# Merging a gMLP out projection into the following attention and projecting Q/K in token chunks: a four-layer kernel on one Trainium2 core

## The chip, the core and the metric

The kernel runs on one core of a Trainium2 chip. The metric is device time in microseconds (us), median of several runs, lower is better. The kernel before takes 1348.54 us (1347.62 to 1350.77, four runs).

TensorE does matmuls, VectorE, ScalarE and GpSimd do elementwise work, and SyncE only issues DMAs. Each of these engines works through its own queue of instructions. A DMA is issued by one of the queues of SyncE, GpSimd or ScalarE. The profile marks a queue as SPq (SyncE), POOLq (GpSimd) or ACTq (ScalarE).

## The reference, cut to what matters

Four layers alternate, A B A B, over x of shape 2048 x 576. A is attention with 32 heads of width 18, where each row attends to 8 rows, two apart. B is a gated MLP with a spatial matmul.

```python
def A(x):                                    # x = x + A(layernorm(x))
    q, k, v = split(x @ wqkv)                # 576 -> 3 * 576
    # row s attends to rows s, s-2, ..., s-14; softmax; times v
    return o @ wo

def B(x):                                    # x = x + B(layernorm(x))
    z = gelu(x @ w_in)                       # 576 -> 4608
    z1, z2 = z[..., :2304], layernorm(z[..., 2304:])
    g = w_sp @ z2 + b_sp                     # [2048, 2048] @ [2048, 2304]
    return (z1 * g) @ w_out                  # 2304 -> 576
```

## The kernel before

Activations are kept normalised and transposed in `xnT` (features on partitions). Five stages follow each other:

1. Attention 1. Rows are handled in 19 tiles of 112, each with a halo of 16 earlier rows, and each tile in two halves of 16 heads: 38 steps.
2. z2 projection (16 tiles of 128 rows) and spatial matmul (18 feature blocks) of the first B.
3. Out projection of the first B, then attention 2.
4. z2 projection and spatial matmul of the second B.
5. Out projection of the second B, and the output.

Q and K come out of the projection with seven heads stacked in one staging tile. The logits need each head at its own partition offset, so a small DMA per head copies it there. Q/K are made in two blocks of 1024 rows: 64 such copies per attention, dealt to three queues.

```python
# PG: project 512 columns of Q or K; when a block of 1024 is complete, copy each head
for j7 in range(nh):                             # 7 heads (4 in the last group)
    dst_ap = QK[32 * rg:32 * rg + DH, :, g, PADL + cb_c0:PADL + cb_c0 + cb_w]
    src_ap = stg[r0 + DH * j7:r0 + DH * (j7 + 1), :, 0:cb_w]
    # in the steps: SyncE, GpSimd and ScalarE in turn; before them: SyncE and GpSimd
    ...

for s in range(NSTEP):                           # 38 steps
    EXP(s); MASK(s)                              # ScalarE, VectorE
    L_mm(s + 1)                                  # logits of the next step, high priority
    PV(s - 1); NORM(s - 1)                       # values, division
    for fn in table.get(s, []): fn()             # projections, row tails, filler matmuls
```

The tail of a tile (in `table`) is a chain through several engines. SyncE transposes the attention output by DMA, TensorE multiplies by `wo`, and VectorE adds the residual and takes the statistics. GpSimd then normalises, and SyncE transposes into `xnT`.

```python
nc.sync.dma_start_transpose(out=oT_t[:, :, :nq], in_=o_t[:nq, :])          # TAIL_A
...                                                                        # TAIL_B: wo, add, stats
nc.sync.dma_start_transpose(out=self.xnT[:, :, ...], in_=xn[:nrows, :])    # TAIL_C
```

Late steps also hold two filler ("junk") matmuls each, whose results are not used. The z2 norm is nine instructions per tile of rows (six on VectorE, three on GpSimd). W_out is loaded in 18 pieces: all of it after the first spatial stage, and the second half of it after the second.

The softmax here doesn't subtract the row's maximum and nothing guards it: scores larger than these inputs give would overflow.

## Time and profile before

The first view sums each engine's busy time in the five stages. Its columns are the window (us) and its length, then busy us with the count of instructions for TensorE, its weight loads, VectorE, ScalarE and GpSimd, and last the mean granted TensorE clock, the busy share of the DMA engines and GB/s.

```profile
...
core 0: us, PE busy (x) PEld busy (x) DVE busy (x) ACT busy (x) POOL busy (x), PEclk, DMA share, GB/s
0.00:188.00 188.00, 143.74 (x1840) 85.66 (x1841) 121.92 (x314) 96.77 (x130) 101.97 (x147) 0.96 0.68 141
188.00:605.00 417.00, 407.00 (x1912) 186.45 (x1911) 167.69 (x355) 92.68 (x165) 73.63 (x93) 1.00 0.16 35
605.00:849.00 244.00, 218.37 (x2421) 143.49 (x2420) 143.55 (x347) 101.93 (x135) 94.34 (x135) 0.95 0.65 151
849.00:1264.00 415.00, 407.32 (x1909) 186.84 (x1908) 167.57 (x354) 92.79 (x165) 73.13 (x93) 1.00 0.16 35
1264.00:1348.00 84.00, 73.47 (x580) 57.01 (x577) 15.75 (x34) 0.00 (x0) 13.36 (x21) 0.95 0.33 101
...
```

TensorE is busy in 407 of 417 us of a z2 and spatial stage. The room lies in the two attention stages (144 of 188 us and 218 of 244 us) and in the last stage.

Next come the waits of TensorE, one line for each thing waited for: total us, number of times, longest. First attention 1:

```profile
...
PE pw L582 <- DMA oT_142<-o_t_129: 4.0, 1, 4.0
PE pp L412 <- DMA xnT<-ln_xn_84: 3.3, 1, 3.3
...
```

the start of the z2 stage:

```profile
...
PE pz L812 <- DMA win2b<-in_B_w_in_dram: 3.6, 1, 3.6
...
```

and the out projection of the first and the second B:

```profile
...
PE po_6066 L941 <- DMA wout_b<-in_B_w_out_dram: 7.1, 6, 2.1
...
```

```profile
...
PE po_12694 L941 <- DMA wout_b<-in_B_w_out_dram: 3.0, 3, 1.0
```

So W_out arrives late twice and a part of the z2 weights once per stage. These are the waits that the change sets out to remove.

The last two views concern DMA issue. The first gives minimum/median/maximum duration in ns of one Q/K copy issue on SyncE, and the second a stretch of SyncE's queue in attention 1 (start, duration, queue, line, operation, count).

```profile
...
L76 SPq DMA_DIRECT2D QK<-stg x48: 786/787/1016, 38.3 to 773.5; - x48
...
```

```profile
...
104.49 1.23 SPq L568 DMA_TRANSPOSE oT_142<-o_t_131  x1
105.77 0.57 SPq L76 DMA_DIRECT2D xo<-in_A_x_dram  x1
106.44 2.51 SPq L76 DMA_DIRECT2D QK<-stg  x3
110.22 1.22 SPq L186 DMA_TRANSPOSE xnT<-ln_xn_84  x1
...
```

A copy holds the queue for 787 ns and a transpose for 1.2 us.

### The profile page before, as it was taken

Reading aid. Unit: us, or ns where it says so; the run is one execution under the profiler, and the core shown is the slowest. Engines: PE = TensorE matmul, PEld = TensorE weight load, DVE = VectorE, ACT = ScalarE, POOL = GpSimd, SP = SyncE. Lnnn points to the kernel's source line nnn. Section 1 sums busy time; section 2 is a strip of 40 time slices with the busy share of each in tenths; the row PEclk is TensorE's granted clock in tenths of the full one; section 3 lists DMA queues with packets and bytes.
Section 4 is the critical chain, followed back from the end, with each engine's and each line's share of the span. In section 5 each row is a group of like instructions: output and inputs, shape, how many; then the busy total and the mean of one; then the engine's idle time right before and its main releaser. Section 6 shows DMA issues by size and latency. Waiting matters only on the chain.

```text
span 1348.4 us, 21451 instructions
## 1 busy us (share of the span) xinstructions
PE 1249.9 (93%) x8656; PEld 659.5 (49%) x8656; DVE 616.5 (46%) x1402; ACT 384.2 (28%) x595; POOL 356.4 (26%) x487
## 2 busy tenths in 40 slices
PE   1999969989999999998998987899999999999997
PEld 0456644434444444445754655444444444444576
DVE  4468858843322332332534878588323223333221
ACT  2556726620011111001126665465101111100000
POOL 7445547830000000002141646488000000000111
PEclk9999989999999999997999999899999999999999
DMA  9449759020000000009653677861100000000232
GB/s 264 98 94 145 121 134 214 1 90 6 9 10 9 10 9 9 0 4 266 179 137 62 151 145 129 181 125 41 43 9 9 10 9 9 2 7 1 72 113 67
DMA packets 180128, 101.04 MB, mean 75 GB/s; under 512 B 138276, under 2 KB 162212, under 8 KB 180028
## 3 DMA queue, kind: packets, MB, share of 16 engines
q1 hardware_dynamic: 170208, 84.15, 28.1%
q10 hardware_dynamic: 6364, 8.55, 2.2%
q0 software_dynamic: 3456, 6.96, 2.2%
q8 instruction: 68, 1.11, 0.3%
q14 instruction: 32, 0.26, 0.1%
HBM read 41.16 MB, written 16.52 MB: 43 GB/s over the span
## 4 chain that ended last, share of the span: by engine, by line
PE 62%; DVE 11%; POOL 10%; issue 7%; DMA 6%; ACT 3%; SPq 1%; ACTq 0%; POOLq 0%; DVEq 0%
PE pg L904 36%; PE po L941 9%; DVE z_junkD L819 4%; PE pp L412 3%; DMA QK<-stg 2%; POOL ln_xn_84 L181 2%; POOL ln_xn_81 L181 1%; POOL ln_rstd L164 1%; POOL z_rstd L835 1%; POOL ln_xn_83 L181 1%; POOL ln_xn_82 L181 1%; DMA wout_b<-in_B_w_out_dram 1%; DMA wv_sb<-in_A_wqkv_dram 1%; DMA win2b<-in_B_w_in_dram 1%; DVE z_msq L828 1%
## 5 line engine op out<-in xcount | busy, mean ns | idle before, releaser
L908 DVE TENSOR_TENSOR g_tmp<-pg,bsp 128x512 f32<-128x512 f32 x144 | 99.4, 692 | 435.5 <-PE pg L904 423.9
L412 PE MATMUL pp<-xnT,wqk_sb 128*128 128x512 bf16 x400 | 100.7, 394 | 29.8 <-DMA xnT<-ln_xn_84 28.5
L812 PEld LDWEIGHTS <-xnT 128*128 128x128 bf16 x800 | 78.4, 98 | 97.0 <-issue 13.0
L812 PE MATMUL pz<-win2a,xnT 128*128 128x512 bf16 x384 | 103.1, 379 | 5.9 <-ACT zp L816 4.4
L164 POOL TENSOR_TENSOR ln_rstd<-ln_rstd,neg_half 112x1 f32<-112x1 f32 (+2 forms) x70 | 43.4, 621 | 152.3 <-DVE ln_rstd L163 152.1
L812 PE MATMUL pz<-win2b,xnT 128*128 128x512 bf16 x256 | 77.0, 386 | 6.9 <-DMA win2b<-in_B_w_in_dram 6.9
L816 ACT ACTIVATE zp<-pz 128x1024 bf16<-128x1024 f32 x64 | 65.0, 1020 | 44.6 <-POOL z2b_9746 L845 18.9
L412 PEld LDWEIGHTS <-wqk_sb 128*128 128x128 bf16 x400 | 36.9, 100 | 71.2 <-issue 36.0
L819 DVE CUSTOM_DVE_ANT_0 z_junkD<-zp 128x1536 bf16<-128x1536 bf16 x32 | 56.9, 1777 | 18.7 <-ACT zp L816 18.7
L370 PE MATMUL pv<-wv_sb,xnT 128*128 128x288 bf16 (+1 forms) x380 | 62.2, 286 | 0.2 <-DVE stg L418 0.2
L76 POOL DMA_DIRECT2D wout_b<-in_B_w_out_dram x14 | 7.5, 541 | 172.4 <-PE pg L904 172.4
L76 POOL DMA_DIRECT2D QK<-stg x52 | 31.5, 608 | 73.0 <-ACT stg L420 28.0
L584 DVE TENSOR_TENSOR x_new<-pw,xo 112x288 f32<-112x288 f32 (+1 forms) x76 | 33.5, 445 | 18.0 <-PE pw L582 10.7
L420 ACT CAST stg<-pp 128x512 bf16<-128x512 f32 x54 | 31.0, 585 | 37.4 <-PE pp L412 22.7
L370 PEld LDWEIGHTS <-xnT 128*128 128x128 bf16 (+1 forms) x380 | 33.5, 97 | 15.8 <-issue 1.4
L489 PE MATMUL L_ps<-QK 18*128 18x112 bf16 (+1 forms) x1216 | 32.0, 210 | 4.9 <-DMA QK<-stg 1.7
L418 DVE CAST stg<-pp 128x512 bf16<-128x512 f32 x26 | 18.0, 691 | 37.0 <-PE pp L412 33.5
L159 DVE BATCH_NORM_STATS2 ln_st<-x_new 112x6 f32<-112x288 f32 (+1 forms) x76 | 33.9, 449 | 1.2
L489 PEld LDWEIGHTS <-QK 18*128 18x128 bf16 (+1 forms) x1216 | 20.4, 93 | 25.6 <-issue 21.6
L845 POOL TENSOR_SCALAR z2b_3101<-zp,z_rstd,z_nmr 128x256 bf16<-128x256 bf16 x16 | 32.4, 2024 | 0.0
L845 POOL TENSOR_SCALAR z2b_9746<-zp,z_rstd,z_nmr 128x256 bf16<-128x256 bf16 x16 | 32.4, 2023 | 0.0
L904 PE MATMUL pg<-W_sb,z2b_3093 128*128 128x512 bf16 x128 | 28.4, 379 | 1.9 <-DVE z2b_3093 L848 1.9
(549 smaller groups left out, 2513.3 us busy)
## 6 DMA issues: line engine op xcount, KB each, us to landing
xres_73<-x_new SPq DMA_DIRECT2D x18, 252.0 KB
xo<-xres_74 SPq DMA_DIRECT2D x18, 252.0 KB
xres_75<-x_new SPq DMA_DIRECT2D x18, 252.0 KB
QK<-stg POOLq DMA_DIRECT2D x52, 72.0 KB, 3.8
win2a<-in_B_w_in_dram SPq DMA_DIRECT2D x2, 1728.0 KB
QK<-stg SPq DMA_DIRECT2D x48, 72.0 KB
wqk_sb<-in_A_wqkv_dram ACTq DMA_DIRECT2D x4, 576.0 KB
out_dram<-ob SPq DMA_DIRECT2D x16, 144.0 KB
```

The source lines that it names most:

```text
L164: nc.gpsimd.tensor_tensor(out=rstd[:nrows, :], in0=rstd[:nrows, :], in1=self.neg_half[:nrows, :], op=ALU.pow)
L181: e.tensor_scalar(out=xn[:nrows, 0:D], in0=x_t[:nrows, :], scalar1=mv[:nrows, 0:1], scalar2=rstd[:nrows, 0:1], op0=ALU.subtract, op1=ALU.mult)
L370: nc.tensor.matmul(pv[:nk, 0:288], lhsT=self.xnT[:, c, QT * t:QT * t + nk], rhs=wv_sb[:, c, hh * 288:(hh + 1) * 288], start=(c == 0), stop ...
L412: nc.tensor.matmul(pp[:, :], lhsT=wqk_sb[:, c, wc0:wc0 + P], rhs=self.xnT[:, c, col0:col0 + 512], start=(c == 0), stop=(c == 4))
L489: nc.tensor.matmul(L_ps[:nk, j, ftl * QT:ftl * QT + nq], lhsT=kT[32 * j:32 * j + DH, g, QT * t:QT * t + nk], rhs=qT[32 * j:32 * j + DH, g, ...
L812: nc.tensor.matmul(pzvs[ci][:, sub * 512:sub * 512 + w], lhsT=self.xnT[:, c, PADL + i * P:PADL + (i + 1) * P], rhs=win2(c)[:, c0 + sub * 5 ...
L816: nc.scalar.activation(out=zp[:, c0:c0 + cn], in_=pzvs[ci][:, 0:cn], func=ACT.Gelu_apprx_tanh, accum_out=sums[:, ci:ci + 1])
L819: nc.vector.tensor_tensor_reduce(out=junkD[:], in0=zp[:, 0:SQ_D], in1=zp[:, 0:SQ_D], scale=1.0, scalar=0.0, op0=ALU.mult, op1=ALU.add, acc ...
L845: nc.gpsimd.tensor_scalar(out=z2b[b][:, i, :], in0=zp[:, b * 256:(b + 1) * 256], scalar1=rstd[:, 0:1], scalar2=nmr[:, 0:1], op0=ALU.mult, ...
L904: nc.tensor.matmul(pg[:, :], lhsT=z2b[jj][:, i, sub * P:(sub + 1) * P], rhs=W_sb[:, i, q * 512:(q + 1) * 512], start=(i == 0), stop=(i == ...
L908: nc.vector.tensor_tensor(out=tmp[:], in0=pg[:, :], in1=bsp[:, q * 512:(q + 1) * 512], op=ALU.add)
L941: nc.tensor.matmul(acc[hh], lhsT=uT[j // 2][:, j % 2, i * P:(i + 1) * P], rhs=wout_j(j)[:, hh * 288:(hh + 1) * 288], start=(j == 0), stop= ...
```

## The change

The intent is to fill TensorE's idle time. The out projection of the first B becomes 16 units (one per 128 rows). Units 0 to 4 run ahead of the steps of attention 2 and units 5 to 15 inside steps 0 to 20. That needs Q/K in small token chunks, since a chunk can be projected once its rows exist. There are five chunks of 3, 4, 4, 4 and 4 tiles, each with its halo. The z2 data moves to four tiles `zc`, one per 512 rows. The product z1 * g overwrites z2 one block behind, and Q/K chunks reuse the part that is free. W_out and the z2 weights now load whole and early, the z2 norm is one VectorE instruction, the filler is gone, and the last layer writes bf16 straight from the add.

The core of the diff (cut; renamings and reordering left out):

```diff
-    def __init__(self, S=2048, F=4608, layers="ABAB", njunk=2, cb_widths=(1024,), prio=200, prio2=0):
+    def __init__(self, S=2048, F=4608, layers="ABAB", CT=(3, 4, 4, 4, 4), prio=200):
...
+        self.zc = [c.tile([P, 4, (cfg.NB + 1) * 256], bf16, name=f"zc{q}") for q in range(cfg.NQ)]
...  # Q/K chunks in freed zc tiles
+        for c in range(1, NC):
+            w = HALO + chunks[c][3]
+            flat = self.zc[c - 1][:].rearrange("p a b -> p (a b)")
+            QK.append(flat[:, 0:16 * w].rearrange("p (a g w) -> p a g w", a=2, g=8))
...  # one unit of the out projection, placed in the prologue or in a step
+                        po = self.PT_tile("po")
+                        self.p3_mm(i, hh, po)
+                        nc.vector.tensor_tensor(out=x3[:, hh * 288:(hh + 1) * 288], in0=po[:, 0:288],
+                                                in1=xo3[:, hh * 288:(hh + 1) * 288], op=ALU.add)
...  # copies: 32 per chunk, five chunks
-                        if in_steps:
-                            r = dma_rr[0] % 3      # SyncE, GpSimd, ScalarE
...
+                        self.dma(QK[c][32 * rg:32 * rg + DH, :, g, :], stg[r0 + DH * j7:r0 + DH * (j7 + 1), :, 0:w],
+                                 eng=(nc.gpsimd if stg_rr[0] % 3 == 0 else nc.sync))
...
-            table.setdefault(s_, []).append(JUNK(cfg.njunk))
...  # z2 norm
-            for b in range(NB):
-                if b >= NB - NPOOL_NORM:
-                    nc.gpsimd.tensor_scalar(out=z2b[b][:, i, :], in0=zp[:, b * 256:(b + 1) * 256], ...)
-                else:
-                    nc.vector.tensor_scalar(out=z2b[b][:, i, :], in0=zp[:, b * 256:(b + 1) * 256], ...)
+            nc.vector.tensor_scalar(out=zc[i // 4][:, i % 4, 256:256 + Fh], in0=zp[:], scalar1=mean[:, 0:1],
+                                    scalar2=rstd[:, 0:1], op0=ALU.subtract, op1=ALU.mult)
...  # W_out: whole, at the third feature block of the spatial stage
+            if jj == 2:
+                load_wout()
...  # last stage: bf16 from the add
+                nc.vector.tensor_tensor(out=ob[:, hh * 288:(hh + 1) * 288], in0=po[:, 0:288],
+                                        in1=xo[:, hh * 288:(hh + 1) * 288], op=ALU.add)
```

Copies per attention go from 64 on three queues to 160 on two, two thirds of them on SyncE.

## The prediction

> **What bounds the kernel now.** The slice table and the busy time per stretch show four stages per pair of layers.
> (1) Attention: 0-187 us and 689-848 us. Late, a tile (two steps) takes 5.7 us; VectorE is busy 4.3-4.8 of every 5 us (mask 1.1 us, residual adds and statistics 4 x 0.45 us per tile); TensorE runs filler matmuls (88 x 0.22 us = 19 us).
> (2) z2 projection, 187-279 us and 848-938 us: 5.01 us per tile of 128 rows on TensorE, 16 tiles = 80 us, so about 11 us are lost.
> (3) Spatial matmul, 326 us twice, TensorE at full rate with no gap: 18.13 us per feature block in the chain of waits.
> (4) Out projection, 605-689 us and 1265-1340 us: 576 matmuls x 0.1225 = 70.6 us. The first loses about 13 us, the second 5 us, to late W_out and the half clock after it; then an 8 us tail.
>
> **What changes, costed.**
> - W_out prefetched, bf16 written by the add itself, no cast: the last stage loses its 5 us and a little of the tail: -5 us.
> - z2 weights wholly prefetched: the waits of 3.6-3.9 us on the late two fifths at each z2 start vanish. One VectorE op replaces six of 0.34-0.43 us and three on GpSimd (0.6, 0.6, 2.0 us). The Trainium skill ("VectorE: DVE Perf Modes", perf-mode tier table) lists a bf16 tensor_scalar of 2048 elements at 693 ns; estimate 0.8-0.9 us for 2304; no run shows it. TensorE waited only 2 us for this norm: -6 us per z2 stage, -12 in all, mainly the weights.
> - Middle out projection in the attention: 70.6 us of TensorE move into a stage that has about 120 us of useful TensorE work in 160 us. But they bring VectorE 16 x 2.1 us = 34 us. Summing the larger of the two per step gives about 175 us of steps after about 40 us of prologue and before 10 of tail: 225-235 us against 243 us now: -15 us.
> - Q/K in chunks: 5 x 32 = 160 copies per attention instead of 64, 107 of them on the SyncE queue. One takes 0.79 us of issue there, a DMA transpose 1.2 us. SyncE then holds about 175 us of issue in an attention of 187 us, 190 in the merged one. This nearly cancels the gain of an earlier start (first exponential at about 42 instead of 52 us) and the removed filler: first attention 0 us, between -15 and +12.
>
> **Sum.** 0 - 12 - 15 - 5 = -32: 1316 us, 8 in 10 between 1285 and 1345. Faster by over 2%: 0.56; within 2%: 0.40; slower by over 2%: 0.04.
>
> **What would show it.** Right: spatial stages still 326 us each; the z2 stages 81-84 us, norm op below 1 us; last stage 71-73 us plus 6 us; in both attentions SyncE's issue blocks nearly back to back, and the waits of the logits matmuls on Q/K copies grow from 2-5 us to over 10. Wrong: first attention ended before 175 us, or merged stage below 205 us.
>
> **What would make it wrong.** SyncE's in-order queue blocking transposes behind copies: +20 us per attention. False dependencies of z2 and its overwritten blocks in one buffer: a stall per block would cost over 100 us. Without filler the clock may fall: "TensorE: Matmul & The Clock Gate", HAM oscillation, says that idle gaps above about 3.4 us halve it; this trace shows 0.66-0.71 after such gaps.

## The result, and the profile after

The changed kernel takes 1405.88 us (1405.32 to 1408.9, four runs) and is correct. The ratio to the kernel before is 1.0427 (95% interval 1.0408 to 1.0447), so it is 4.3% slower. A ratio is the mean time of one kernel's fast runs over that of the other's in the same rounds, so it is not quite the ratio of the medians. Where kernels from different sets are compared below, I use their ratios times 1348 us.

The stages are bounded here by the first z2 matmul, the first out projection matmul, and so on, read from the trace in us:

| stage | before | after | change |
|---|---|---|---|
| attention 1 | 188.1 | 221.6 | +33.5 |
| z2 + spatial, first | 417.2 | 415.4 | -1.8 |
| out projection + attention 2 | 243.3 | 281.4 | +38.1 |
| z2 + spatial, second | 415.9 | 411.0 | -4.9 |
| last stage | 83.9 | 74.1 | -9.8 |

The busy times by stage, columns as before, from windows that begin and end on whole us:

```profile
...
0.00:222.00 222.00, 154.92 (x1847) 94.11 (x1848) 123.56 (x321) 104.02 (x156) 109.21 (x154) 0.85 0.52 124
222.00:637.00 415.00, 405.03 (x1874) 187.39 (x1910) 152.43 (x274) 95.34 (x166) 13.95 (x29) 0.99 0.16 36
637.00:918.00 281.00, 228.47 (x2422) 152.66 (x2423) 143.91 (x351) 104.08 (x156) 104.35 (x132) 0.86 0.52 132
918.00:1329.00 411.00, 404.84 (x1874) 187.42 (x1911) 152.82 (x275) 95.33 (x166) 13.31 (x23) 0.99 0.16 36
1329.00:1403.00 74.00, 70.73 (x576) 56.28 (x576) 15.71 (x34) 0.00 (x0) 0.00 (x0) 1.00 0.32 97
...
```

Both attention stages grew, and the granted clock in them fell from 0.96 and 0.95 to 0.85 and 0.86. TensorE's busy time rose by only 11 us and 10 us; the rest of the growth is time in which it stood idle. The DMA engines were not fuller: their busy share in the two attention stages fell from 0.68 and 0.65 to 0.52.

TensorE's waits in attention 1:

```profile
...
PE pw L435 <- DMA oT_113<-o_t_110: 6.4, 2, 4.4
PE pw L435 <- DMA oT_112<-o_t_109: 5.1, 2, 3.8
PE L_ps L377 <- DMA zc_68<-stg: 4.7, 4, 1.9
PE pp L328 <- DMA xnT<-ln_xn_72: 4.6, 1, 4.6
...
PE L_ps L377 <- DMA qk_101<-stg: 2.5, 3, 1.0
...
```

The transposes (`oT`, `xnT`) come first. Waits of the logits on copies (the lines with `L_ps` and a DMA; three short ones are cut here) sum to 9.0 us, not to more than 10. In the middle stage it is the transposes again, 23.1 us in these three lines against 6.2 us for `oT` in the kernel before:

```profile
...
PE pw L435 <- DMA oT_5979<-o_t_5976: 11.1, 4, 3.9
PE pw L435 <- DMA oT_5980<-o_t_5977: 6.3, 1, 6.3
PE pw L435 <- DMA oT_5981<-o_t_5978: 5.7, 2, 2.9
...
```

SyncE issues these transposes. Its queue in attention 1, and the duration of a copy issue:

```profile
...
90.59 3.34 SPq L65 DMA_DIRECT2D zc_69<-stg  x4
94.04 1.23 SPq L154 DMA_TRANSPOSE xnT<-ln_xn_73  x1
95.36 4.15 SPq L65 DMA_DIRECT2D zc_69<-stg  x5
99.62 1.21 SPq L65 DMA_DIRECT2D xres_80<-x_new  x1
100.94 1.26 SPq L424 DMA_TRANSPOSE oT_113<-o_t_110  x1
102.25 0.57 SPq L65 DMA_DIRECT2D xo<-in_A_x_dram  x1
102.93 4.16 SPq L65 DMA_DIRECT2D zc_69<-stg  x5
...
```

```profile
...
L65 SPq DMA_DIRECT2D zc_69<-stg x42: 786/787/979, 81.2 to 788.1; - x42
...
```

The copy still takes 787 ns, although it moves less than half as many columns. But now four or five copies stand together, 3.3 to 4.2 us long, and a transpose that becomes ready behind them waits, because the queue keeps its order. One case, from VectorE's timeline:

```profile
...
97.36 0.44 DVE L414 TENSOR_TENSOR o_t_110<-O_ps,rec 112x288 bf16<-112x288 f32 x1
...
```

This write completes the attention output of a tile at 97.80 us. SyncE was then in a block of five copies, and issued the transpose of that output at 100.94 us. For tiles 4 to 18 of attention 1 the median time from such a write to the issue of its transpose is 3.78 us, against 0.16 us in the kernel before (worked out from the timelines of VectorE and SyncE).

The issue durations add up to 150.0 us in 28 to 193 us, a share of 0.91 (89.9 us of it copies); over 28 to 221 us, to the end of the stage, the share is 0.85. In the middle stage it is 0.70, against 0.63 in the kernel before.

The parts that were meant to gain:

```profile
...
L611 DVE TENSOR_SCALAR zc_68<-zp,z_mean,z_rstd x8: 878/879/880, 232.1 to 942.6; 128x2304 bf16<-128x2304 bf16 x8
...
```

```profile
...
PE pz_4021 L647 <- DMA w_0_4015<-in_B_w_in_dram: 6.9, 1, 6.9
```

The z2 norm takes 879 ns in one instruction, and the last stage no longer waits for W_out. But a new wait of 6.9 us for the first z1 weights stands between the z2 and the spatial part. In the second B it is 3.1 us. The kernel before waits 1.8 and 2.6 us there.

### The profile page after: what moved, and what is told of

Same layout as the page of the kernel before. It is cut to its first block, busy times and chain, and to the rows that moved or that the text cites. A ratio compares the mean times of both kernels' runs of the same rounds, so it can differ in the third digit from the quotient of the medians.

```text
span 1403.5 us, 21530 instructions
## 1 busy us (share of the span) xinstructions
PE 1264.0 (90%) x8592; PEld 677.9 (48%) x8668; DVE 588.4 (42%) x1252; ACT 398.8 (28%) x644; POOL 240.8 (17%) x335
## 4 chain that ended last, share of the span: by engine, by line
PE 77%; DMA 7%; issue 5%; POOL 4%; SPq 3%; DVE 2%; ACT 2%; ACTq 0%; DVEq 0%; POOLq 0%
PE pg L658 34%; PE pz L584 10%; PE po L213 9%; PE pp L328 5%; SPq L65 2%; PE pw L435 2%; PE pv L353 2%; PE L_ps L377 1%; PE O_ps L403 1%; PE pzs L584 1%; POOL ln_rstd L133 1%; DMA oT_5979<-o_t_5976 1%; DMA w_0_4015<-in_B_w_in_dram 1%; POOL ln_xn_74 L149 1%; POOL ln_xn_75 L149 1%
## 5 line engine op out<-in xcount | busy, mean ns | idle before, releaser
L328 PE MATMUL pp<-xnT,wqk_sb 128*128 128x464 bf16 (+2 forms) x500 | 120.1, 380 | 43.2 <-DMA xnT<-ln_xn_74 25.1
L658 PE MATMUL pg<-W_sb,zc_68 128*128 128x512 bf16 x570 | 147.9, 380 | 0.1
L658 PE MATMUL pg<-W_sb,zc_70 128*128 128x512 bf16 x560 | 146.3, 379 | 1.3
L658 PE MATMUL pg<-W_sb,zc_71 128*128 128x512 bf16 x564 | 146.2, 379 | 0.7
L658 PE MATMUL pg<-W_sb,zc_69 128*128 128x512 bf16 x560 | 146.3, 379 | 0.6
L658 PEld LDWEIGHTS <-zc_71 128*128 128x128 bf16 x576 | 56.4, 98 | 68.7 <-DVE zc_71 L611 1.0
L658 PEld LDWEIGHTS <-zc_68 128*128 128x128 bf16 x576 | 56.6, 98 | 68.2 <-issue 1.1
L658 PEld LDWEIGHTS <-zc_69 128*128 128x128 bf16 x576 | 56.5, 98 | 68.3 <-issue 0.6
L658 PEld LDWEIGHTS <-zc_70 128*128 128x128 bf16 x576 | 56.4, 98 | 67.7
L328 PEld LDWEIGHTS <-wqk_sb 128*128 128x128 bf16 x500 | 48.1, 103 | 84.3 <-issue 52.9
L133 POOL TENSOR_TENSOR ln_rstd<-ln_rstd,neg_half 112x1 f32<-112x1 f32 (+2 forms) x70 | 47.5, 679 | 196.7 <-DVE ln_rstd L132 184.7
L584 PE MATMUL pz<-win_127,xnT 128*128 128x512 bf16 x312 | 72.0, 382 | 1.2 <-DVE x_new L437 0.5
L584 PE MATMUL pz<-win_9026,xnT 128*128 128x512 bf16 x312 | 71.8, 381 | 1.1 <-DVE x_new L437 0.5
L353 PE MATMUL pv<-wv_sb,xnT 128*128 128x288 bf16 (+1 forms) x380 | 65.6, 307 | 2.0 <-ACT v_ext_104 L360 2.0
L334 ACT CAST stg<-pp 128x464 bf16<-128x464 f32 (+2 forms) x68 | 34.3, 515 | 57.0 <-PE pp L328 40.2
L353 PEld LDWEIGHTS <-xnT 128*128 128x128 bf16 (+1 forms) x380 | 36.9, 104 | 16.8 <-issue 4.0
```

The source lines that it names most:

```text
L133: nc.gpsimd.tensor_tensor(out=rstd[:nrows, :], in0=rstd[:nrows, :], in1=self.neg_half[:nrows, :], op=ALU.pow)
L328: nc.tensor.matmul(pp[:, 0:w], lhsT=Aw["wqk"][:, k_, wc0:wc0 + P], rhs=self.xnT[:, k_, lo:lo + w], start=(k_ == 0), stop=(k_ == 4))
L334: nc.scalar.copy(out=stg[:, qk, 0:w], in_=pp[:, 0:w])
L353: nc.tensor.matmul(pv[:nk, 0:288], lhsT=self.xnT[:, c, QT * t:QT * t + nk], rhs=Aw["wv"][:, c, hh * 288:(hh + 1) * 288], start=(c == 0), s ...
L584: nc.tensor.matmul(pz[:, k_ * 512:k_ * 512 + w], lhsT=lhs[c], rhs=win2[:, c, c0:c0 + w], start=(c == 0), stop=(c == 4))
L658: nc.tensor.matmul(pg[:, :], lhsT=zc[i // 4][:, i % 4, f0:f0 + P], rhs=W_sb[:, i, q * 512:(q + 1) * 512], start=(i == 0), stop=(i == NS - 1))
```

## The experiments

Five theories were open after reading the traces:

- T1, issue: the 160 copies fill in-order queues, and the transposes and row loads behind them come late.
- T2, clock: without filler, TensorE falls to a lower clock in the attention.
- T3, merge: the out projection inside the attention costs more than it saves.
- T4, bunching: the projections of a chunk are squeezed into too few steps.
- T5, norm: the single long VectorE instruction holds up other work.

Every run is the changed kernel with one edit, unless said otherwise, and has four runs. The results together:

| run | median us | ratio to before (95%) | attention 1 | middle stage |
|---|---|---|---|---|
| before | 1348.54 | 1 | 188.1 | 243.3 |
| after | 1405.88 | 1.0427 (1.0408-1.0447) | 221.6 | 281.4 |
| qk_sync | 1470.24 | 1.0911 (1.0890-1.0931) | 259.0 | 303.3 |
| qk_pool | 1398.42 | 1.0378 (1.0361-1.0396) | 220.6 | 276.3 |
| qk_3way | 1379.97 | 1.0227 (1.0202-1.0252) | 208.7 | 268.3 |
| nocopy (wrong result) | 1353.67 | 1.0023 (0.9998-1.0048) | 191.0 | 261.7 |
| filler | 1409.16 | 1.0460 (1.0444-1.0475) | 217.0 | 282.2 |
| spread | 1408.88 | 1.0440 (1.0420-1.0460) | 218.4 | 284.9 |
| norm_split | 1410.75 | 1.0481 (1.0456-1.0506) | 220.7 | 283.7 |
| unmerge | 1392.71 | 1.0336 (1.0320-1.0351) | 219.9 | 266.8 |
| nocopy_unmerge (wrong result) | 1328.27 | 0.9865 (0.9835-0.9895) | 189.7 | 234.8 |
| hybrid | 1332.50 | 0.9894 (0.9874-0.9914) | 189.1 | 242.0 |
| hybrid_hp | 1332.23 | 0.9891 (0.9869-0.9914) | 187.9 | 242.2 |
| nocopy_filler (wrong result) | 1375.20 | 1.0203 (1.0178-1.0227) | 202.6 | 267.9 |
| nocopy_pv (wrong result) | 1368.13 | 1.0142 (1.0112-1.0171) | 196.4 | 264.5 |
| nocopy_win2split (wrong result) | 1353.89 | 1.0034 (1.0002-1.0066) | 187.4 | 257.7 |

The stage columns come from the one profiled execution of each kernel, so differences of a few us in them carry little weight. The profiled execution of nocopy was its slowest, 1359.22 us, so its stages come out some us long.

### Who issues the copies: qk_sync, qk_pool, qk_3way

```diff
-  eng=(nc.gpsimd if stg_rr[0] % 3 == 0 else nc.sync))
+  eng=nc.sync)                                                # qk_sync
+  eng=nc.gpsimd)                                              # qk_pool
+  eng=(nc.sync, nc.gpsimd, nc.scalar)[stg_rr[0] % 3])         # qk_3way
```

> The opposite dose: all 160 Q/K copies of each attention on SyncE, 53 more than in the kernel after. Theory 1: 53 x 0.83 us = 44 us more issue per attention; the first attention, whose queue is nearly full, grows by 30 to 44 us, the merged one by 15 to 44; total 1450 to 1490 us. Theories 2 and 3: within 10 us of 1406.

> The kernel after, with all 160 Q/K copies of each attention issued from GpSimd instead of a third of them. Theory 1 (SyncE's in-order issue queue holds the attentions): SyncE loses 107 x 0.83 us = 89 us of issue per attention, its share in the first attention falls from 0.91 to under 0.5, the first attention ends 20 to 40 us earlier (first z2 matmul at 185 to 200 us instead of 222), the merged stage shrinks by 20 to 40 us; total 1330 to 1365 us. Theory 2 (the clock falls because the filler matmuls are gone): total within 10 us of 1406. Theory 3 (the out projection's work collides with the attention's on VectorE and TensorE): only the first attention gains, the merged stage stays at 270 us or more.

> The kernel after, copies dealt in turn to SyncE, GpSimd and ScalarE, a third each. Theory 1: SyncE has 53 x 0.83 = 44 us less issue per attention, GpSimd as before, ScalarE 43 us more where it was busy 55%: total 1360 to 1390 us. Theory 4 (order of work): within 10 us of 1406, or slower as ScalarE's exponentials wait.

The copies are the same in all three, with the same bytes and the same destinations. Only the issuing queue differs, and with it the time of one issue (0.59 us on GpSimd, 0.79 us on SyncE, 0.80 us on ScalarE). The kernel's time goes from 1470 to 1380 us. With all copies on SyncE its share of issue time is 0.96 (183.6 us of 192, 28 to 220 us) and the kernel is 65 us slower than the change itself. With three queues it is 0.70 and the kernel gains 27 us on the change. Both totals lie in the ranges expected under T1. The delay of the transposes follows the dose: the median from the write of an attention output to the issue of its transpose (tiles 4 to 18 of attention 1) is 11.65 us in qk_sync, 3.78 us in the changed kernel and 1.16 us in qk_3way.

Taking all copies off SyncE lowers its share to 0.44, but gains only 7 us. The expectation under T1, 1330 to 1365 us, missed. GpSimd's timeline shows why:

```profile
...
84.11 3.57 POOL L65 DMA_DIRECT2D zc<-stg  x6
87.70 0.96 POOL L133 TENSOR_TENSOR ln_rstd<-ln_rstd,neg_half 128x1 f32<-128x1 f32 x1
88.67 2.29 POOL L149 TENSOR_SCALAR ln_xn<-x_new,ln_mv,ln_rstd 112x576 bf16<-112x576 f32 x1
...
91.16 4.19 POOL L65 DMA_DIRECT2D zc<-stg  x7
...
```

Now GpSimd has blocks of six and seven copies, 3.6 and 4.2 us long, and its own part of the tail (`ln_rstd`, `ln_xn`) stands between them. The windows view counts GpSimd's copy issues as busy time: over 28 to 220 us it shows 155.4 us of 192, against 96.2 us in the changed kernel. From VectorE's last part of a row's statistics to the `ln_rstd` on GpSimd that follows, the median delay in attention 1 after 60 us is 3.6 us, against 0.09 us in the changed kernel. So SyncE is not special: the copies hurt in whichever in-order queue also carries a link of the tail's chain.

### No copies after the first chunk: nocopy

```diff
-  for j7 in range(nh):
+  for j7 in range(nh if c == 0 else 0):
...  # logits read the first chunk's Q/K again, so the result is wrong on purpose
-  k0 = QT * (t - chunks[c][0])
+  k0 = QT * ((t - chunks[c][0]) % 3); c = 0
```

> Wrong result on purpose: the kernel after, in which the Q/K copies of chunks 1 to 4 are left out and every logits matmul reads chunk 0; the projections, their evictions and all else stay. 128 of 160 copies per attention are gone from SyncE and GpSimd, with their waits. Theory 1 (issuing the copies, on whichever in-order queue, holds the attentions): first z2 matmul at 170 to 190 us instead of 222, merged stage 215 to 245 us instead of 282; total 1310 to 1340 us. If the attentions stay over 205 and 265 us, the copies are not the cause and the order of work on TensorE is (theory 4).

128 of the 160 copies are gone; projections, evictions, transposes and row loads all stay. The kernel falls to 1353.67 us, by the ratios 54 us less than the change. 30.6 us of it are in attention 1 and 19.7 us in the middle stage. That is less than expected (a total of 1310 to 1340 us, and 215 to 245 us for the middle stage), but both stages stay below the 205 and 265 us that would have spoken against the copies. The median delay of the transposes in attention 1 is 0.08 us. SyncE's share in attention 1 is 0.63, as in the kernel before. In this run the logits also wait for no copied data, and no copy moves data, so it bounds the whole cost of these 128 copies. The three runs above are what ties it to issue, T1. Of the 54 us, 27 us come back by issuing the same copies on three queues; the other 27 us are not split further.

### Clock, bunching and norm: filler, spread, norm_split

```diff
+  for s_ in range(29, NSTEP):          # filler: two 512-column matmuls in each late step
+      put(s_, JUNK)
-  lo = max(2, hi - 4) if c > 1 else 2
+  lo = max(2, hi - 7) if c > 1 else 2  # spread: projections of a chunk over eight steps, not five
...                                     # norm_split: the nine instructions of before
```

> The kernel after, with two filler matmuls of 512 columns per step put back from step 29 on, as the kernel before had them. Theory 2 (lost filler, half clock): granted clock in the late steps rises to 1.0 and the total falls by 10 to 30 us. Theory 1: late steps wait on transposes in the SyncE queue; total within 6 us of 1406, either way.

> The kernel after, with the ten Q/K projections of a chunk spread over the eight steps before it is needed instead of five. Theory 4 (projections bunched in five of eight steps hold TensorE, and the copies come in bunches): total falls by 10 to 30 us. Theory 1: SyncE issues the same sum of copies, only less bunched: 0 to -10 us.

> The kernel after with the z2 norm in nine pieces again, six on VectorE and three on GpSimd, as before. The prediction counted 6 us per z2 stage for norm and weights together, mainly for the weights. If TensorE bounds that stage in either form, the total changes by less than 5 us (1401 to 1411); if the norm held it, by 6 to 20 us.

The filler raises the clock in attention 1, though not to the expected 1.0. Late in attention 1, without and with the edit (column before the last two: granted clock):

```profile
...
180.00:205.00 25.00, 19.59 (x303) 12.21 (x305) 17.15 (x42) 12.36 (x18) 9.54 (x7) 0.74 0.46 112
205.00:222.00 17.00, 9.79 (x95) 5.79 (x93) 8.90 (x29) 1.51 (x3) 7.19 (x7) 0.54 0.41 100
...
```

```profile
...
180.00:205.00 25.00, 22.13 (x341) 13.90 (x342) 19.44 (x50) 12.83 (x20) 9.80 (x8) 0.90 0.46 113
205.00:217.00 12.00, 7.05 (x62) 4.48 (x60) 6.91 (x20) 0.27 (x1) 6.37 (x6) 0.72 0.51 130
217.00:222.00 5.00, 4.95 (x25) 2.42 (x25) 0.79 (x3) 1.47 (x3) 0.79 (x2) 1.00 0.32 55
...
```

With the filler attention 1 ends at 217.0 us, so the window after that belongs to the z2 stage. Within the attention the clock rises from 0.74 and 0.54 to 0.90 and 0.72, and at the end of attention 2 (900 to 918 us) from 0.50 to 0.59. The kernel gets no faster: 1409.16 us. This is not the whole of the old filler: the run has 36 such matmuls, the kernel before 88. And filler takes TensorE time itself, so a gain of a few us from the clock could hide in it. But nocopy, without any filler, ends attention 1 at 191.0 us, within 2.9 us of the kernel before. So T2 falls as an explanation of the loss. The Trainium skill ("TensorE: Matmul & The Clock Gate", section "HAM oscillation — how this bites in real kernels") tells how waits for DMA let the clock fall again; this trace agrees that the clock falls beside such waits (0.54 in the changed kernel after 205 us, where TensorE waits 4.4 us for a transpose), but raising it brought no measured gain here.

Wider spreading of the projections gives nothing either (1408.88 us), so T4 falls as far as it concerns the projections. The edit hardly reached the copies: after the first chunks they still stand in blocks of four or five in SyncE's queue, and the median delay of the transposes is 3.77 us. Bunching of the copies was not tested by itself. Going back to nine norm instructions costs 7 us by the ratios and 5 us by the medians (1410.75 us), so the single instruction is a gain and T5 falls.

### Without the merge: unmerge and nocopy_unmerge

```diff
-  NPRE = min(NS, need[0] + 3)
+  NPRE = min(NS, need[0] + 3) if first else NS   # all 16 units ahead of the steps
```

> The kernel after, with all 16 row tiles of the middle out projection run ahead of the second attention instead of spread over its steps; everything else stays. Theory 3 (merging collides): the stage falls from 282 to about 245 us, total 1365 to 1375. Theory 1: SyncE has the same issues to make, the attention part then takes as long as the first one's, 180 us, after 70 us of projection and some 20 of start: the total changes by 0 to -15 us, so 1390 to 1406.

> Wrong result on purpose: copies of chunks 1 to 4 left out as in nocopy, and the middle out projection run ahead of the attention as in unmerge. nocopy's merged stage took 262 us against 243 for the two stages of the kernel before. If merging by itself costs (theory 3), this stage is 10 to 20 us shorter than 262 and the total 1335 to 1345 us. If merging pays once the copies are gone (what the prediction assumed), this stage is 15 us or more longer than 262 and the total above 1368 us.

With the copies in place, taking the merge out gains 12 us. 1392.71 us lies in the range expected under T1, not under T3. Without the copies it gains 21 us by the ratios and 25 us by the medians (1328.27 against 1353.67 us), more than expected under T3. So T3 holds as a second cause. In both, the middle stage is shorter: 266.8 against 281.4 us and 234.8 against 261.7 us. The prediction had put the merge at a gain of 15 us. The middle stage by windows, merged (nocopy), then not merged (nocopy_unmerge):

```profile
...
607.00:680.00 73.00, 59.70 (x507) 40.10 (x506) 28.28 (x66) 22.41 (x32) 12.57 (x31) 0.88 0.50 140
680.00:800.00 120.00, 108.08 (x1256) 76.35 (x1256) 71.64 (x177) 52.75 (x79) 39.92 (x37) 0.96 0.50 122
800.00:868.00 68.00, 50.47 (x673) 33.10 (x663) 43.11 (x109) 28.94 (x45) 27.58 (x18) 0.75 0.54 120
...
```

```profile
...
605.00:680.00 75.00, 70.00 (x544) 53.92 (x545) 31.80 (x86) 13.57 (x20) 17.26 (x45) 0.98 0.67 184
680.00:800.00 120.00, 111.32 (x1502) 74.17 (x1500) 85.39 (x196) 75.82 (x115) 46.56 (x33) 0.99 0.55 123
800.00:840.00 40.00, 26.39 (x382) 17.09 (x381) 26.41 (x71) 14.22 (x22) 16.77 (x13) 0.71 0.52 112
...
```

Not merged, the out projection runs at 70 busy us of 75, and the central 120 us of the attention keep TensorE busy for 111 us at a clock of 0.99. There was no room of a quarter to be filled there. Merged, the first exponential comes earlier, at 650.8 instead of 691.9 us, but the steps take 203 us (to 854.2) instead of 134 us (to 825.7). That is 69 us more for eleven units whose matmuls take 11 x 4.41 = 48.5 us outside (70.6 us over 16 units). Summed over the windows, merging adds 10.5 us of busy time (218.3 against 207.7 us) and 15.5 us of idle time (42.7 against 27.3 us). The excess lies in steps 0 to 20, which hold the units: by the start times of the exponentials they take 139.9 us merged and 77.0 us not merged, 62.9 us more for 48.5 us of matmuls. Steps 21 to 37 take 63.8 and 57.1 us (58.3 us in nocopy_win2split, also merged). The last windows differ mainly in how much work falls in them, 673 and 382 matmuls. Rows of the out projection are needed in order, so all units sit in steps 0 to 20 and none are left for the late steps. That this order is the cause is not shown: it is read from the kernel's text, and no run moved units into later steps.

### What the merge's cost is not: nocopy_filler, nocopy_pv, nocopy_win2split

These were run to find the cause of those 21 to 25 us. Each is nocopy with one more edit.

```diff
+  for s_ in range(5, NSTEP): put(s_, JUNK)             # nocopy_filler
+  with pr(cfg.prio // 2): PV(s - 1); NORM(s - 1)       # nocopy_pv: value matmuls ahead of the units
+  for c in range(5): put(s26 + 2 * c, piece(c))        # nocopy_win2split: z2 weights in five pieces
```

> Wrong result on purpose: nocopy with two filler matmuls in every step from 5 on, in both attentions. If the half clock in the gaps is what makes the merged stage 27 us longer than the unmerged one (262 against 235), the clock goes to 1.0 and the total falls 5 to 20 us below 1354. If the gaps are waits and TensorE is full between them, the filler's 33 x 0.43 = 14 us per attention adds 5 to 25 us.

> Wrong result on purpose: nocopy with the value matmuls and the normalisation given half the logits matmuls' priority, so that they stand before the projections of the step in TensorE's order. If the merged stage is long because the softmax chain waits behind 2.2 us blocks of out projection in order, the total falls by 10 to 25 us; if TensorE is simply full in these steps, within 6 us of 1354.

> Wrong result on purpose: nocopy with the 2.65 MB of z2 weights for the second gMLP loaded in five pieces two steps apart instead of in one burst. In the merged stage of the kernel after, a transpose issued beside that burst took 8.1 us to land and TensorE waited for it. If the burst is part of the merge's 27 us, the total falls by 4 to 10 us; otherwise within 3 us.

More filler costs 24 us against nocopy, within the 5 to 25 us expected if TensorE is full between its waits. Its own matmuls come to an estimated 28 us (14 us per attention, as in the expectation), and it raises the clock of the late steps only to 0.83, so a few us from the clock are not excluded; that it explains all 21 to 25 us has no support. Priority for the value matmuls costs 16 us, which fits neither branch of its expectation: this order is worse, and why stays open. Loading the z2 weights in pieces changes nothing clear of noise: 1353.89 against 1353.67 us, with overlapping intervals, although the load of the z2 weights (issued at 834.9 and 847.9 us in the changed kernel) falls beside a transpose that took 8.14 us from issue to landing. What exactly makes a merged step longer than its parts stays open.

### What is worth keeping: hybrid and hybrid_hp

The kernel before keeps its attention and its separate out projection. It takes from the change the `zc` layout, the one-instruction norm, the whole W_out loaded in the spatial stage, the two-DMA z1 weight load and the bf16 add. Space then forces the weights of attention 2 to load at its own start. hybrid_hp raises the priority of those loads. The first part of the z2 weights is still loaded ahead and the rest late, as in the kernel before.

```diff
-  z2b = [zu.tile([P, NS, 256], bf16, ...) for b in range(NB)]
+  zc = [zu.tile([P, 4, (NB + 1) * 256], bf16, name=f"zc{q}") for q in range(NQ)]
...
+  nc.vector.tensor_scalar(out=zc[i // 4][:, i % 4, 256:256 + Fh], in0=zp[:], ...)
...
+  if jj == 2:                                   # whole W_out, spatial stage
+      self.dma(wout[:, 0:h, :], wv_[:, 0:h, :], eng=nc.gpsimd)
+      self.dma(wout[:, h:, :], wv_[:, h:, :], eng=nc.gpsimd)
-  late_loads.append(self.open_A_weights(li + 1, defer="all"))
...
+  with tc.high_priority(offset=600):            # hybrid_hp only
+      self.open_A_weights(li, defer=False)
```

> A kernel meant to be faster than both: the attention and the separate middle out projection of the kernel before (two blocks of 1024 tokens, 64 copies, three queues), with the z2 layout, the one-op norm, the whole prefetch of W_out and the bf16 result straight from the add taken from the kernel after. Counting stage by stage from the two traces: last stage 84 to 74 us, late W_out ahead of the middle projection -13 us, second attention's weights now loaded at its own start +6 us, z2 stages -2 us each: total 1320 to 1335 us.

> As hybrid, with the loads of the second attention's weights given a higher priority in the order of instructions, so that they are issued during the middle out projection: the +6 us of hybrid falls to about 0: 0 to 6 us below hybrid.

Both are correct and beat both kernels: 1332.50 and 1332.23 us, 1.1% less than before, which is clear of 1 by its interval. The gain is in the last stage (74.2 us, 9.7 less) and the two z2 and spatial stages (413.2 and 412.9 us, 4.0 and 3.0 less). The middle stage hardly moves (242.0 us), though W_out is no longer late. The waits of hybrid_hp show what took its place:

```profile
...
PE pp L414 <- DMA wqk_sb<-in_A_wqkv_dram: 6.2, 1, 6.2
PE pp L414 <- issue: 4.5, 2, 4.3
```

The wait for W_out, 7.1 us before, became a wait for the Q/K weights of 6.2 us. In hybrid it is 7.4 us: the priority hardly moved it, and the 0.3 us between the two medians are within noise.

## Why the prediction was wrong

The prediction was 1316 us, the result 1405.88 us: the sign was wrong. Point by point:

- **First attention, "0 us, between -15 and +12": wrong, +33.5 us.** This is the step that failed first. The parts were read correctly: 0.79 us for a copy issue, 107 copies on SyncE, and an earlier first exponential (40.2 us against 51.7 us in the traces). The failure was to compare a sum of issue time (175 us) with the span (187 us) and to call it even. A queue that is 91% full (28 to 193 us) and in order doesn't only have to fit in the span. It also delays the transposes behind its copies (median 3.78 us instead of 0.16 us), and the chain of a tile goes through it twice. nocopy puts the copies of attention 1 at 31 us. The prediction did name this risk, as "+20 us per attention", but left it out of the sum.
- **Merge, "-15 us": wrong, +38.1 us in that stage.** By nocopy about 20 us of it are copies. By unmerge and nocopy_unmerge the merge itself costs 12 to 25 us where a gain was expected. The claim of 120 us of useful TensorE work in 160 us counted on 40 us of room. In the kernel before it was 127.5 of 159 us (690 to 849 us, 141.2 us busy less 13.7 us of filler); in the middle of the attention, unmerged and without copies, 9 of 120 us were idle. The prediction counted 175 us of steps; merged they took 225 us in the changed kernel (679.7 to 904.5 us, first to last exponential) and 204 us without the copies. Summing the larger of two engines per step left out the waits between steps; which of these waits the merge adds stays open.
- **z2, "-12 us": mechanism right, size off.** Both z2 and spatial stages together gained 6.7 us in the profiled execution. In the other runs with the same z2 code they gained 0.7 to 6.4 us, so about half of the size predicted is the most that can be claimed. The waits of the z2 weights are gone and the norm takes 879 ns, where 0.8 to 0.9 us was estimated. The new waits for z1 weights (6.9 and 3.1 us, against 1.8 and 2.6 us) give back 5.6 us. hybrid loads these weights by the same two DMAs and waits 1.0 us in the first B, so their number is not the cause.
- **Last stage, "-5 us": better, -9.8 us.** The waits for W_out went, as said. The tail shortened as well, from the 8 us that the prediction read to 3.3 us (74.1 less 70.75 us of out projection), where only "a little" was expected.
- **Logits waiting over 10 us for copies: wrong.** They waited 9.0 us in attention 1. More of the delay showed up at the transposes (11.5 us on `oT` and 7.0 us on `xnT`).
- **SyncE's blocks back to back: right** (0.91 in attention 1). **False dependencies of z2 and its overwritten blocks: none**; a feature block still takes 18.13 us.
- **Clock: it fell, as feared, but is not what the kernel lost its time to.** filler raised it in part and gained nothing, and nocopy recovered attention 1 without filler.

## What to carry to other kernels

Before adding many small DMAs, sum their issue time per queue and ask what else stands in that queue. Keep a queue that carries transposes or loads of a critical chain well below full, and deal out the copies in small groups over several queues rather than in bunches on one. Before moving matmuls into another stage to fill its idle time, look at the windows in which they would land: idle time summed over a stage need not lie where the order of rows puts them. When a bundle of changes fails, take it apart; here the prefetches and the simpler instructions were worth some 15 us, hidden under a far larger loss.

## What the Trainium skill lacked or had wrong

- "DMA: Bandwidth & Descriptors", section "Issuing engines are not separate DMA queues", says that issuing on several engines saves only the issue time on the sequencer, "which is usually small relative to the DMA itself". Here it was not small. A copy held SyncE for 0.787 us and GpSimd for 0.59 to 0.62 us; those of GpSimd landed 2.1 to 2.4 us (medians) after issue, and the trace gives no landing time for SyncE's. With 160 of them per attention the choice of issuer alone moved the kernel from 1470 us (one queue) to 1380 us (three queues).
- The same page, section "Anatomy of one DMA — SWDGE (gpsimd) path", gives about 50 ns for the sequencer's dispatch and calls the descriptor generation after it "small, variable". A copy issued by GpSimd held its queue for 0.59 to 0.62 us in these traces, which do not split the two. For this chip the page gives no duration of an issue on SyncE by shape, which would have served here: 0.787 us for a copy of 18 partitions, the same for 1024 and for 464 columns in each of two rows; 0.34 to 0.53 us (medians) for a row load or store; 1.2 us for a transpose of 112 x 640.
- "VectorE: DVE Perf Modes", section "The perf-mode tier table (the rule you actually need)", gives 693 ns for a `tensor_scalar` of 2048 bf16 elements. In proportion that would be 780 ns for 2304 elements (an estimate from the page's figure); 879 ns were measured here, 13% more.
- "TensorE: Matmul & The Clock Gate", section "HAM oscillation — how this bites in real kernels", names restructuring the loop and padding as cures. I found no page that says what matmuls added only to hold the clock up bring or cost: here they raised it from 0.74 to 0.90 in a late window, and the kernel took 1409 us instead of 1406 us.
